# Attention values stored unscaled beside their reciprocals, gathered rows scaled before the transposes, and a new order of the attention

## Chip, cores and metric

The kernel runs on one core of a Trainium2 chip. The metric is the device time of one execution in microseconds; the median of three runs is compared. TensorE runs at one of two clock levels, 1.2 or 2.4 GHz; the profile gives the granted clock as a share of 2.4.

## What is computed

Eight batches of eight heads: 512 tokens x and 32 state rows attend to each other, both ways. The results are rows of 512 numbers (4608 rows). Each row goes to one of eight experts, greedily by its gate logits with room for 576 rows in each, and then through a gated network that all rows share:

```python
xread = np.matmul(softmax(scale * x @ state.T), state)
sread = np.matmul(softmax(scale * state @ x.T), x)
logits = x @ w_gate
out[mask] = np.maximum(x[mask] @ w1[e], 0.0) @ w2[e]
return (silu(x @ w_gate) * (x @ w_val)) @ w_out
```

The softmax divides by its sum plus 1e-9.

## The kernel before

The attention is written as 343 short steps, each a function of a batch (and a half or quarter); the string ORDER lists them, `name.batch`, and a loop issues them so that each step's instructions stand behind those of the step before on every engine:

```python
    for op in ORDER.split():
        name, b = op.split(".")
        in_order(DO[name], int(b))
```

The names: x (TensorE transposes a quarter of the tokens) and ax (its copy into xT, by VectorE or ScalarE as X_VECTOR says); p, ap and q, aq (state and its gate columns; aq copies into SC); z (scores), m, n, y, o (maxima and block transposes); c or C (subtraction of the row maximum, zc, on POOL or VectorE); e, E and f (exponentials of the two softmaxes); t, at (transposes of one of them); r, ar (token values into px, copied to xu with their sums and gate parts); s (state values), S0 (sum plus 1e-9 and reciprocal, rd), S1 (scaled state values ss, stored to DRAM by SP); d (reciprocals of the token sums), M (token values times reciprocals into xm, in two halves on POOL, then stored to xm_d by SP, line 429), w (gate logits of the tokens into Lw, on POOL); G, aG, GG, aGG (transposes of ss, copy into TS, gate products of the state rows, copy into Lw). Batch 7 is read in two halves (A, B1, l0, LB, l1, w1). N, I and cnt make the keys of all 34 columns of 128 rows, the comparison table for the first digit in five pieces (CHUNKS), and its 34 products. The values of batches 7 and 6 are scaled behind the list by ScalarE, 64 instructions (lines 487 to 507).

Then `search` and `place` find, digit by digit, which rows go to the first expert, and write their numbers to idx. POOL gathers these rows from xm_d, five tiles of up to 128 rows (line 916); TensorE transposes each tile (`turn`, line 925), ScalarE and VectorE split it into a high and a low part xh, xl (lines 930 and 931). The first expert's weights come from DRAM as soon as its number is known; ScalarE makes their high parts (line 1132), VectorE the remainders (line 1142); beside them VectorE makes the keys of the next search. Twenty products of no use run on TensorE in between (`spin`).

The experts take 128 units, 16 to an expert: twelve products into one of two PSUM tiles h, an activation on ScalarE (hh, line 950), a remainder on VectorE (hl, line 951), and twelve products of an earlier unit. A table `plan` says at which unit other work is issued: the selection for the next expert, its weights, gathers ("g"), transposes ("t"). Instructions of one engine then run in the order in which the compiler's scheduler puts them within such pins (`issue_after`). Behind the experts the shared network runs for the rest of the time.

## Time and profile before

| | us |
|---|---|
| median of three runs | 1329.91 |
| lowest and highest | 1327.9, 1331.71 |
| the profiled execution | 1332.65 |
| its span, first to last instruction | 1330.9 |
| TensorE busy in the span | 1289.3 (97%) |
| VectorE, ScalarE, POOL busy | 1039.9, 544.0, 409.4 |

The rows below are from this one execution. A group of instructions has its line, engine, operation, output and inputs, the count, the busy time with the mean in ns, and behind a bar the engine's idle time ahead of it with what ended it. In a timeline the first number is the start in us from the span's start, the second the duration, and the square bracket is the idle time ahead and its releaser. PE is TensorE, DVE VectorE, ACT ScalarE; line 245 stands for all steps of the attention, which one helper records.

### The profile page before, as it was taken

To read this page: it belongs to the slowest core of one execution; us is meant where nothing else is said; L and a number is where in the kernel's file an instruction comes from. 1 tells how busy PE (TensorE), PEld (TensorE's weight loads), DVE (VectorE), ACT (ScalarE), POOL (GpSimd) and SP (SyncE) were. 2 spreads that over 40 slices of the span, in tenths; PEclk is the share of its full clock that TensorE was granted. 3 is DMA by queue.
4 is the path that set the end of the run, shared out by engine and by line. 5 is a ranking of instruction groups with operands and counts; after the bars stand their busy time and mean duration, and the time that the engine had idled before them with its cause. 6 is when DMAs were issued, how large, how long until landed. Compare 5 with 4: busy or idle time off the path is not lost.

```text
span 1330.9 us, 28488 instructions
## 1 busy us (share of the span) xinstructions
PE 1289.3 (97%) x11113; PEld 1253.9 (94%) x11113; DVE 1039.9 (78%) x2040; ACT 544.0 (41%) x1047; POOL 409.4 (31%) x349
## 2 busy tenths in 40 slices
...
GB/s 185 225 127 168 119 98 219 150 117 216 155 138 153 198 142 195 93 269 214 161 175 172 285 212 206 278 234 204 293 180 202 176 239 129 172 170 133 131 124 64
DMA packets 129782, 236.97 MB, mean 178 GB/s; under 512 B 29168, under 2 KB 55792, under 8 KB 128624
## 3 DMA queue, kind: packets, MB, share of 16 engines
...
## 4 chain that ended last, share of the span: by engine, by line
PE 90%; DVE 5%; DMA 2%; ACT 1%; issue 1%; SPq 0%; POOLq 0%; DVEq 0%; ACTq 0%
PE b L1257 53%; PE h L946 15%; PE y L962 5%; PE y L965 5%; PE y L961 5%; PE pt L245 2%; PE px L245 2%; PE bt L925 1%; PE acc L642 1%; DMA xc<-in_x_dram 1%; DMA yr<-m_d 1%; PE z L245 1%; PE acc L734 0%; DMA raw<-in_moe_w_dram 0%; DVE m L1307 0%
## 5 line engine op out<-in xcount | busy, mean ns | idle before, releaser
L1257 PE MATMUL b<-yb,w 128*128 128x364 f32 (+1 forms) x3024 | 500.5, 327 | 1.7 <-DVE m L1303 1.5
L1257 PEld LDWEIGHTS b<-yb,w 128*128 128x128 f32 x3024 | 499.5, 188 | 2.6 <-DVE m L1303 2.1
L1257 PE MATMUL b<-w,yb 128*128 128x256 f32 x2160 | 256.3, 281 | 0.9 <-ACT yb L986 0.6
L1257 PEld LDWEIGHTS b<-w,yb 128*128 128x128 f32 x2160 | 255.7, 188 | 1.4 <-ACT yb L986 0.9
L946 PE MATMUL h<-xh,w 128*128 128x288 f32 (+1 forms) x1024 | 207.9, 295 | 1.5 <-ACT xh L930 1.2
L946 PEld LDWEIGHTS h<-xh,w 128*128 128x128 f32 x1024 | 161.6, 189 | 2.5 <-ACT xh L930 1.8
L916 POOL DMA_INDIRECT xg<-xm_d,idx x38 | 49.6, 1304 | 354.6 <-PE bt L925 155.7
L946 PE MATMUL h<-xl,w 128*128 128x288 f32 (+1 forms) x512 | 147.8, 291 | 0.5 <-DVE xl L931 0.5
L961 PE MATMUL y<-hh,w 128*128 128x288 f32 (+1 forms) x512 | 136.0, 291 | 0.1
L962 PE MATMUL y<-hh,w 128*128 128x288 f32 (+1 forms) x512 | 135.7, 291 | 0.0
L950 ACT ACTIVATE hh<-h 128x288 fp32r<-128x288 f32 (+1 forms) x128 | 50.9, 398 | 187.8 <-PE h L946 176.4
L1304 ACT ACTIVATE m<-m 128x364 f32<-128x364 f32 (+1 forms) x108 | 54.8, 507 | 156.5 <-DVE m L1303 151.1
L987 DVE TENSOR_TENSOR yb<-ty,yb 128x512 fp32r<-128x512 f32 (+2 forms) x96 | 92.0, 964 | 12.8 <-ACT yb L986 10.9
L961 PEld LDWEIGHTS y<-hh,w 128*128 128x128 f32 x512 | 96.5, 189 | 0.3 <-ACT hh L950 0.3
L946 PEld LDWEIGHTS h<-xl,w 128*128 128x128 f32 x512 | 96.0, 188 | 0.9 <-DVE xl L931 0.9
L962 PEld LDWEIGHTS y<-hh,w 128*128 128x128 f32 x512 | 96.5, 189 | 0.0
L951 DVE SCALAR_TENSOR_TENSOR hl<-h,hh 128x288 fp32r<-128x288 f32 (+1 forms) x128 | 55.7, 436 | 50.2 <-ACT hh L950 49.8
L1014 POOL TENSOR_TENSOR tt<-raw 128x512 f32<-128x512 f32 (+1 forms) x23 | 30.8, 1341 | 207.3 <-DMA raw<-m_d 154.6
L986 ACT CAST yb<-ty 128x512 fp32r<-128x512 f32 (+2 forms) x96 | 66.6, 694 | 56.5 <-PE b L1257 28.7
L965 PE MATMUL y<-hl,w 128*128 128x288 f32 (+1 forms) x512 | 88.0, 290 | 0.0
L987 DVE TENSOR_TENSOR yb<-yr,yb 128x512 fp32r<-128x512 f32 (+2 forms) x73 | 75.6, 1037 | 10.0 <-ACT yb L986 9.3
L1307 DVE TENSOR_TENSOR m<-cv,m 128x364 f32<-128x364 f32 (+1 forms) x108 | 68.9, 638 | 9.6 <-ACT m L1304 0.2
...
## 6 DMA issues: line engine op xcount, KB each, us to landing
...
```

Of the source, the lines that this page charges most:

```text
L245: done = getattr(getattr(nc, self.name), op)(*args, **kwargs)
L946: hooks["p"] = nc.tensor.matmul(ph, W[i][0][k][q == 1][:, fs], (xl if q == 2 else xh)[:, k, :T], start=(n == 0), stop=(n == 11)).ins
L950: relu[16 * i + 8 * hf + f] = hooks["hh"] = nc.scalar.activation(hh, ph, AF.Relu).ins
L951: lower[16 * i + 8 * hf + f] = hooks["h"] = nc.vector.scalar_tensor_tensor(hl, ph, 0.0, f32(hh), op0=OP.max, op1=OP.subtract).ins
L961: nc.tensor.matmul(p[d], wh[:, f % 2, ds_], hh, start=(f == 0), stop=False)
L962: nc.tensor.matmul(p[d], wl[:, f % 2, ds_], hh, start=False, stop=False)
L965: nc.tensor.matmul(p[d], wh[:, f % 2, ds_], hl, start=False, stop=(f == 7))
L986: nc.scalar.copy(hi, src)
L987: nc.vector.tensor_tensor(lo, src, f32(hi), OP.subtract)
L1257: nc.tensor.matmul(out, a, b, skip_group_check=True, start=start and n == 0, stop=stop and n == len(terms) - 1)
L1304: hooks["silu"] = nc.scalar.activation(m[:, l], m[:, l], AF.Silu).ins
L1307: hooks["gate"] = nc.vector.tensor_tensor(m[:, l], c, m[:, l], OP.mult).ins
```

## The change

Rows of xm_d become 8 x 73 numbers instead of 8 x 64: a head's 64 unscaled values, the reciprocal of its sum in the place of the sum, and its eight gate parts. The steps M and the 64 instructions behind the list go; d stores the whole tile xu, of which there are four now. State rows are stored scaled as before, with ones beside them (one9). Gathered tiles have 584 columns and are multiplied by their reciprocals before the transposes (`scale_rows`): the first expert's first two by VectorE, all others by ScalarE in eight instructions each. The plan issues gathers of tiles 3 and 4 and the transposes at other units. The sum plus 1e-9 of the state rows goes from S0 to a step V on POOL; aq and aG go from ScalarE to VectorE; for batches 1 to 7 the ax of the last quarter (ax3) goes from VectorE to ScalarE. K makes the keys of the first 24 columns, T0 to T2 three pieces of the table, kc their 24 products; N, I and cnt do the rest. The list has a new order. The first expert's weight remainders are pinned ahead of and between the two VectorE scalings, the next keys behind them.

```diff
@@ -51,26 +51,26 @@
-X_VECTOR = (1, 3)
+X_VECTOR = (1,)
 ORDER = """
...
-x0.7 f0.6 at0.5 f1.6 c0.6 c1.6 ax3.7 ax0.7 S0.5 e0.6 r0.5 S0.6 t0.6 e1.6 ar0.5 z.7 m.7 r1.5 E.6 at0.6
-s0.5 y1.7 t1.6 y0.7 ar1.5 M0.4 s1.5 n.7 w.4 d.5 r0.6 S1.5 at1.6 G.5 f0.7 aG.5 o1.7 C1.7 e1.7 o0.7
-s0.6 t0.7 ar0.6 f1.7 M1.4 s1.6 S1.6 S0.7 r1.6 C0.7 GG.3 aGG.3 at0.7 M1.5 t1.7 E1.7 ar1.6 at1.7 s0.7 M0.5
-A1.7 e0.7 s1.7 G.6 d.6 S1.7 w.5 E0.7 B1.7 w.6 G.7 l1.7 w1.7 A0.7 aG.6 aG.7 GG.7 l0.7 LB.7 aGG.7
-N.7 I.7 cnt.7
...
+x3.6 at0.4 G.2 aG.2 x2.6 x0.6 n.5 ax3.6 ax2.6 o.5 ax0.6 f1.5 f0.5 c1.5 x1.6 r0.4 c0.5 ax1.6 V.4 q.6
+x0.7 aq.6 ax0.7 G.3 e1.5 aG.3 w.1 z.6 q.7 e0.5 m.6 ar0.4 S0.4 t1.4 aq.7 y.6 r1.4 o.6 s0.4 E.5
+at1.4 w.2 x1.7 s1.4 ar1.4 S1.4 n.6 V.5 c1.6 x3.7 ax1.7 f1.6 ax3.7 x2.7 ax2.7 t0.5 G.4 d.3 r0.5 c0.6
+e1.6 f0.6 d.4 at0.5 z.7 aG.4 e0.6 ar0.5 E.6 t1.5 at1.5 t0.6 y1.7 at0.6 r1.5 w.3 m.7 w.4 s0.5 t1.6
+s1.5 y0.7 o0.7 ar1.5 S0.5 at1.6 o1.7 S1.5 n.7 f1.7 d.5 r0.6 V.6 c0.7 c1.7 e0.7 GG.3 ar0.6 aGG.3 s0.6
+G.5 w.5 s1.6 f0.7 e1.7 aG.5 r1.6 E0.7 E1.7 ar1.6 S0.6 S1.6 K.7 t0.7 V.7 at0.7 d.6 T0.7 t1.7 T2.7
+A1.7 s0.7 at1.7 B1.7 S0.7 G.6 w.6 s1.7 l1.7 S1.7 A0.7 G.7 aG.6 T1.7 aG.7 GG.7 kc.7 l0.7 w1.7 LB.7
+aGG.7 N.7 I.7 B0.7 cnt.7
@@ -87,7 +87,7 @@
     dram = ctx.enter_context(tc.tile_pool(name="dram", bufs=1, space=bass.MemoryType.DRAM))
-    xm_d = dram.tile([N, DM], F32, name="xm_d")
+    xm_d = dram.tile([N, H * ROW], F32, name="xm_d")
@@ -136,6 +136,8 @@
     nc.gpsimd.memset(SC[:, :, :, D:D + 1], 1.0)
+    one9 = ac.tile([32, H, ROW - D], F32, name="one9")
+    nc.gpsimd.memset(one9, 1.0)
@@ -278,7 +280,7 @@
     def prep_gate2(b):
-        an.scalar.copy(SC[:, b, :, D + 1:], st[b]["q"][:, :2 * E].rearrange("p (g e) -> p g e", g=2))
+        an.vector.tensor_copy(SC[:, b, :, D + 1:], st[b]["q"][:, :2 * E].rearrange("p (g e) -> p g e", g=2))
@@ -406,28 +408,23 @@
     def xread2(b, half):
...
         if "xu" not in t:
-            t["xu"] = aw.tile([128, 4, H, ROW], F32, name="xu", bufs=3)
+            t["xu"] = aw.tile([128, 4, H, ROW], F32, name="xu", bufs=4)
...
+    def row_store(b, xu, dst):
+        nc.sync.dma_start(dst, xu.rearrange("p r h c -> p r (h c)"))
+    def token_rows(b):
+        return xm_d[b * SE:b * SE + S].rearrange("(p r) c -> p r c", r=4)
     def xscale(b):
         xu = st[b]["xu"]
-        rd = st[b]["rd"] = aw.tile([128, 4, H], F32, name="rd", bufs=2)
+        rd = aw.tile([128, 4, H], F32, name="rd", bufs=2)
         an.vector.tensor_scalar(rd, xu[:, :, :, D], 1e-9, None, op0=OP.add)
-        an.vector.reciprocal(rd, rd)
-    def xmake(b, j):
-        t = st[b]
-        xu, rd = t["xu"], t["rd"]
-        done = "xm" in t
-        if not done:
-            t["xm"] = aw.tile([128, 4, H, D], F32, name="xm")
-        xm, q = t["xm"], slice(2 * j, 2 * j + 2)
-        an.gpsimd.tensor_tensor(xm[:, q], xu[:, q, :, :D], rd[:, q, :, None].to_broadcast([128, 2, H, D]), OP.mult)
-        if done:
-            nc.sync.dma_start(xm_d[b * SE:b * SE + S].rearrange("(p r) c -> p r c", r=4),
-                              xm.rearrange("p r h d -> p r (h d)"))
+        an.vector.reciprocal(xu[:, :, :, D], rd)
+        row_store(b, xu, token_rows(b))
     def add_heads(b, xw):
@@ -435,9 +432,9 @@
     def logits(b):
-        xu, rd = st[b]["xu"], st[b]["rd"]
+        xu = st[b]["xu"]
         xw = aw.tile([128, 4, H, E], F32, name="xw")
-        an.gpsimd.tensor_tensor(xw, xu[:, :, :, D + 1:], rd[:, :, :, None].to_broadcast([128, 4, H, E]), OP.mult)
+        an.gpsimd.tensor_tensor(xw, xu[:, :, :, D + 1:], xu[:, :, :, D:D + 1].to_broadcast([128, 4, H, E]), OP.mult)
...
     def read_half(b, j):
@@ -451,8 +448,8 @@
     def keep_half(b):
         t = st[b]
-        t["xh"] = aw.tile([128, 2, H, ROW], F32, name="xu", bufs=3)
-        an.scalar.copy(by_row(t["xh"]), by_bank(t["h", 1]))
+        t["xh", 1] = aw.tile([128, 2, H, ROW], F32, name="xu", bufs=4)
+        an.scalar.copy(by_row(t["xh", 1]), by_bank(t["h", 1]))
     def half_logits(b, j):
@@ -470,41 +467,30 @@
     def gates_sum(b):
...
+    def half_store(b, j):
+        row_store(b, st[b]["xh", j], token_rows(b).rearrange("p (k j) c -> p j k c", j=2)[:, j])
     def kept_scale(b):
-        t = st[b]
-        rd = t["rd", 1] = aw.tile([128, 2, H], F32, name="rd1", bufs=1)
-        an.vector.tensor_scalar(rd, t["xh"][:, :, :, D], 1e-9, None, op0=OP.add)
-        an.vector.reciprocal(rd, rd)
+        xh = st[b]["xh", 1]
+        rd = aw.tile([128, 2, H], F32, name="rd1", bufs=1)
+        an.vector.tensor_scalar(rd, xh[:, :, :, D], 1e-9, None, op0=OP.add)
+        an.vector.reciprocal(xh[:, :, :, D], rd)
+        half_store(b, 1)
     def kept_logits(b):
-        t = st[b]
+        xh = st[b]["xh", 1]
         xw = aw.tile([128, 2, H, E], F32, name="xw")
-        an.gpsimd.tensor_tensor(xw, t["xh"][:, :, :, D + 1:],
-                                t["rd", 1][:, :, :, None].to_broadcast([128, 2, H, E]), OP.mult)
+        an.gpsimd.tensor_tensor(xw, xh[:, :, :, D + 1:], xh[:, :, :, D:D + 1].to_broadcast([128, 2, H, E]), OP.mult)
...
-    def scale_values(b):
+    def values_half(b):
         t = st[b]
-        xm = aw.tile([128, 4, H, D], F32, name="xm")
-        for j in range(2):
-            for k in range(2):
-                for h in range(H):
-                    m = 2 * k + h // 4
-                    v = t["h", 0][:, h % 4, ROW * m:ROW * m + D] if j == 0 else t["xh"][:, k, h, :D]
-                    an.scalar.activation(xm[:, 2 * k + j, h, :], v, AF.Copy, scale=t["rd", j][:, k, h:h + 1])
-        nc.sync.dma_start(xm_d[b * SE:b * SE + S].rearrange("(p r) c -> p r c", r=4),
-                          xm.rearrange("p r h d -> p r (h d)"))
-    def scale_kept(b):
-        xu, rd = st[b]["xu"], st[b]["rd"]
-        xm = aw.tile([128, 4, H, D], F32, name="xm")
-        for r in range(4):
-            for h in range(H):
-                an.scalar.activation(xm[:, r, h, :], xu[:, r, h, :D], AF.Copy, scale=rd[:, r, h:h + 1])
-        nc.sync.dma_start(xm_d[b * SE:b * SE + S].rearrange("(p r) c -> p r c", r=4),
-                          xm.rearrange("p r h d -> p r (h d)"))
+        xh = t["xh", 0] = aw.tile([128, 2, H, ROW], F32, name="xu", bufs=4)
+        an.scalar.copy(by_row(xh), by_bank(t["h", 0]))
+        an.scalar.copy(xh[:, :, :, D], t["rd", 0])
+        half_store(b, 0)
     def sread(b, g):
@@ -519,10 +505,13 @@
...
+    def state_sum(b):
+        den = st[b]["den"] = aw.tile([128, 2], F32, name="den")
+        an.gpsimd.tensor_scalar(den, st[b]["den2"][:, :, 0], 1e-9, None, op0=OP.add)
     def state_scale(b):
         rd2 = st[b]["rd2"] = aw.tile([128, 2], F32, name="rd2")
-        an.vector.tensor_scalar(rd2, st[b]["den2"][:, :, 0], 1e-9, None, op0=OP.add)
-        an.vector.reciprocal(rd2, rd2)
+        an.vector.reciprocal(rd2, st[b]["den"])
     def sread2(b):
@@ -532,8 +521,9 @@
         for h in range(4):
-            dst = xm_d[r0:r0 + NS].rearrange("n (g h d) -> n g h d", g=2, h=4)[:, :, h, :]
+            dst = xm_d[r0:r0 + NS].rearrange("n (g h c) -> n g h c", g=2, h=4)[:, :, h, :D]
             nc.sync.dma_start(dst, ss[32 * h:32 * h + 32])
+        nc.sync.dma_start(xm_d[r0:r0 + NS].rearrange("n (h c) -> n h c", h=H)[:, :, D:], one9)
...
     def sread_gate(b):
@@ -542,7 +532,7 @@
     def sread_gate2(b):
-        an.scalar.copy(TS[:, :, b, :], st[b]["g"][:, :128].rearrange("p (h n) -> p h n", h=4))
+        an.vector.tensor_copy(TS[:, :, b, :], st[b]["g"][:, :128].rearrange("p (h n) -> p h n", h=4))
     def state_gates(b):
@@ -808,20 +798,35 @@
...
+    EARLY_COLUMNS = 24
+    held = {}
+    def early_keys(b):
+        keys(0, EARLY_COLUMNS, True, an)
+        sl["I"] = sel_tile([128, 128 * NC], BF, "I").rearrange("p (g j c) -> p g j c", j=128, c=2)
+    def table(b, j):
+        pairs(sl["I"], 1, Dms[0], *CHUNKS[j], OP.is_le, an)
+    def counts(c0, c1):
+        for c in range(c0, c1):
+            an.tensor.matmul(held["acc"], sl["I"][:, c // 2, :, c % 2], G[:, c, :], start=(c == 0), stop=(c == NC - 1))
+    def early_counts(b):
+        held["acc"] = ap.tile([128, 2, 512], F32, name="z")[:, 0, :E]
+        counts(0, EARLY_COLUMNS)
     def first_keys(b):
-        keys(0, NC, True, an)
+        keys(EARLY_COLUMNS, NC, True, an)
     def first_table(b):
-        sl["I"] = sel_tile([128, 128 * NC], BF, "I").rearrange("p (g j c) -> p g j c", j=128, c=2)
-        for c0, c1 in CHUNKS:
-            pairs(sl["I"], 1, Dms[0], c0, c1, OP.is_le, an)
+        table(b, 3)
+        table(b, 4)
     def first_count(b):
-        acc = ap.tile([128, 2, 512], F32, name="z")[:, 0, :E]
-        for c in range(NC):
-            an.tensor.matmul(acc, sl["I"][:, c // 2, :, c % 2], G[:, c, :], start=(c == 0), stop=(c == NC - 1))
+        counts(EARLY_COLUMNS, NC)
         fe = sl["fe"] = sel_tile([128, E], BF, "fe")
-        an.vector.tensor_tensor(fe, acc, need, OP.is_ge)
+        an.vector.tensor_tensor(fe, held["acc"], need, OP.is_ge)
     def halves(fn, *more):
@@ -829,11 +834,12 @@
           "GG": state_gates, "aGG": state_gates2, "B1": keep_half, "l0": gates_read, "LB": gates_sum,
-          "l1": kept_scale, "w1": kept_logits, "N": first_keys, "I": first_table, "cnt": first_count}
+          "l1": kept_scale, "w1": kept_logits, "N": first_keys, "I": first_table, "cnt": first_count,
+          "B0": values_half, "V": state_sum, "K": early_keys, "kc": early_counts}
...
                            ("t", turn_e2, ()), ("at", turn_e2b, ()), ("s", sread, ()), ("e", exps1, ()),
-                           ("E", exps1b, ()), ("r", xread, ()), ("ar", xread2, ()), ("M", xmake, ()),
+                           ("E", exps1b, ()), ("r", xread, ()), ("ar", xread2, ()), ("T", table, ()),
@@ -842,8 +848,6 @@
             load_x(int(b) + 4)
-    in_order(scale_values, B - 1)
-    in_order(scale_kept, B - 2)
...
@@ -908,17 +913,27 @@
         if i or j < 3:
-            xg = gx.tile([128, DM], F32, name="xg", bufs=3)
+            xg = gx.tile([128, H * ROW], F32, name="xg", bufs=3)
...
             if j == 3:
-                XG["ys"] = bw.tile([128, 4, 288], F32, name="ys", bufs=1).rearrange("p (a b) c -> p a (b c)", a=2)
-            xg = XG["ys"][:, j - 3, :DM]
+                XG["ys"] = bw.tile([128, 4, 292], F32, name="ys", bufs=1).rearrange("p (a b) c -> p a (b c)", a=2)
+            xg = XG["ys"][:, j - 3]
...
                                      in_offset=bass.IndirectOffsetOnAxis(ap=idx[i][:n, j:j + 1], axis=0)).ins
-        XG[i, j] = xg
+        XG[i, j] = xg.rearrange("p (h c) -> p h c", c=ROW)
+    def scale_rows(i, j, eng=None):
+        n = min(128, CAP - 128 * j)
+        xg = XG.pop((i, j))[:n]
+        xs = XS[i, j] = gx.tile([128, H, D], F32, name="xs", bufs=5)
+        if eng is not None:
+            hooks["scaled"] = eng.tensor_tensor(xs[:n], xg[:, :, :D], xg[:, :, D:D + 1].to_broadcast([n, H, D]), OP.mult).ins
+            return
+        for h in range(H):
+            nc.scalar.activation(xs[:n, h, :], xg[:, h, :D], AF.Copy, scale=xg[:, h, D:D + 1])
     def turn(i, j):
-        xg = XG.pop((i, j))
+        xg = XS.pop((i, j)).rearrange("p h d -> p (h d)")
...
@@ -1135,16 +1150,22 @@
         close(0, bpsum)
-    with tc.issue_after(hooks["lw"]):
-        keys(0, NC, False)
-    with tc.issue_after(hooks["key"]):
-        for k in range(4):
-            nc.vector.tensor_tensor(lo[k], first[k], f32(hi[k]), OP.subtract)
+    def first_lower(k, pin):
+        with tc.issue_after(hooks[pin]):
+            hooks["low"] = nc.vector.tensor_tensor(lo[k], first[k], f32(hi[k]), OP.subtract).ins
...
         spin(bp, "y2", 1, P_["spin"])
+    first_lower(0, "lw")
+    first_lower(1, "low")
     for j in range(2):
+        with tc.issue_after(hooks["low"]):
+            scale_rows(0, j, nc.vector)
+        first_lower(2 + j, "scaled")
         turn(0, j)
+    with tc.issue_after(hooks["low"]):
+        keys(0, NC, False)
@@ -1190,10 +1211,13 @@
         for j in range(NT):
-            at(P_["g"][k] + int(j * P_["gs"]), P_["ghook"], gather, k, j)
+            turned = P_["t"][k] + j + 2 * (k == E - 1) if k > 1 else 14 + j + 2 * (j > 2)
+            at(P_["g"][k] + int(j * P_["gs"]) if j < 3 else P_["t"][k] + j - 3 if k > 1 else 17, P_["ghook"] if j < 3 else None, gather, k, j)
+            at(max(turned - 2, P_["g"][k] + 2) if k > 1 else 12 + j if j < 3 else turned - 1, "hh", scale_rows, k, j)
             if k > 1 or j > 1:
-                at(P_["t"][k] + j, P_["thook"], turn, k, j)
+                at(turned, P_["thook"], turn, k, j)
     for j in range(2, NT):
+        at(P_["t0"][j - 2] - 2, "hh", scale_rows, 0, j)
```

## Rows read from the trace of the kernel before

**Rows 1.** Busy time by stretch: TensorE, weight loads, VectorE, ScalarE, POOL, granted clock.
```profile
16.00:77.00 61.00, 57.45 (x1397) 44.75 (x1398) 54.23 (x87) 50.46 (x102) 45.24 (x47) 1.00 0.53 176
77.00:86.00 9.00, 8.90 (x141) 7.50 (x139) 3.10 (x13) 6.37 (x21) 3.89 (x11) 0.52 0.37 133
200.00:300.00 100.00, 100.00 (x990) 97.28 (x990) 82.60 (x219) 36.60 (x65) 11.79 (x10) 1.00 0.48 161
```

**Rows 2.** Groups of VectorE's instructions, 14 to 86 us.
```profile
L245 DVE TENSOR_SCALAR rd<-den 128x2 f32<-128x2 f32 x8 | 5.0, 631 | 0.0
L245 DVE COPY xT<-px 128x512 f32<-128x512 f32 x7 | 4.8, 681 | 1.8 <-ACT e L245 0.7 <-ACT xT L245 0.6 <-ACT nmx L245 0.3
```

**Rows 3.** Groups of POOL's instructions, same stretch.
```profile
L245 POOL TENSOR_TENSOR xm<-xu,rd 128x1024 f32<-128x1024 f32 x12 | 23.4, 1957 | 4.0 <-ACT xT L245 2.6 <-ACT e L245 0.8 <-ACT et L245 0.6
```

**Rows 4.** Groups of ScalarE's instructions, same stretch.
```profile
L245 ACT COPY xT<-px 128x512 f32<-128x512 f32 x7 | 4.1, 589 | 3.0 <-PE px L245 2.9
L245 ACT COPY TS<-pt 128x128 f32<-128x128 f32 x8 | 2.1, 265 | 0.8 <-PE pt L245 0.8
```

**Rows 5.** TensorE's waits, 14 to 90 us: total, times, longest in us.
```profile
PE px L245 <- ACT xT L245: 1.1, 2, 0.7
PE px L245 <- ACT xu L245: 0.9, 3, 0.4
...
PE pt L245 <- DVE ss L245: 0.8, 2, 0.5
...
PE pt L245 <- ACT TS L245: 0.5, 1, 0.5
PE pt L245 <- ACT SC L245: 0.4, 1, 0.4
```

**Rows 6.** Timeline of TensorE near the attention's end: steps s, r and GG.3.
```profile
72.36 0.65 PE L245 MATMUL pt<-xc,et 128*32 128x64 f32 x32
...
74.12 1.13 PE L245 MATMUL px<-SC,e 32*128 32x73 f32 x32
75.78 1.06 PE L245 MATMUL pt<-wgp,TS 128*128 128x8 f32 x8 [0.53 <-DVE ss L245]
```

**Rows 7.** Timeline of VectorE behind the attention: first keys, first table.
```profile
86.22 0.43 DVE L245 TENSOR_REDUCE V<-Lw 128x34 f32<-128x272 f32 x1
...
88.65 2.69 DVE L245 TENSOR_TENSOR I<-IE,Dm 128x1024 bf16<-128x1024 bf16 x5
```

**Rows 8.** Timeline of ScalarE behind the attention: scaling of the last values.
```profile
88.40 8.74 ACT L245 ACTIVATE xm<-xu,rd 128x64 f32<-128x64 f32 x36
```

**Rows 9.** Timeline of POOL: issues of gathers, three of expert 0, one of expert 3.
```profile
113.14 1.18 POOL L916 DMA_INDIRECT xg<-xm_d,idx  x1 [29.53 <-DVE eh L751]
114.62 1.13 POOL L916 DMA_INDIRECT xg<-xm_d,idx  x1 [0.31 <-issue]
116.06 5.77 POOL L916 DMA_INDIRECT xg<-xm_d,idx  x1 [0.30 <-issue]
...
252.83 0.96 POOL L916 DMA_INDIRECT xg<-xm_d,idx  x1 [22.18 <-issue]
```

**Rows 10.** DMA issues, 113 to 114.5 us: median us from issue to landing.
```profile
xg<-xm_d,idx POOLq DMA_INDIRECT x1, 3.6
```

**Rows 11.** Timeline of VectorE behind the first row numbers: Lw, four remainders.
```profile
113.45 0.44 DVE L757 TENSOR_TENSOR Lw<-Lw,dn 128x272 f32<-128x272 f32 x1
...
116.38 4.62 DVE L1142 TENSOR_TENSOR w<-raw,w 128x1024 fp32r<-128x1024 f32 x4
```

**Rows 12.** Timeline of TensorE: the first expert's first products.
```profile
119.58 2.16 PE L946 MATMUL h<-xh,w 128*128 128x256 f32 x16 [0.68 <-ACT xh L930]
122.25 1.20 PE L946 MATMUL h<-xl,w 128*128 128x256 f32 x8 [0.50 <-DVE xl L931]
```

**Rows 13.** Line 950, one activation to a unit: ns, first and last start in us.
```profile
L950 ACT ACTIVATE hh<-h x128: 372/392/417, 123.1 to 558.3; 128x256 fp32r<-128x256 f32 x64, 128x288 fp32r<-128x288 f32 x64
```

**Rows 14.** Groups of ScalarE's instructions, 119 to 500 us.
```profile
L873 ACT CAST w<-raw 128x1024 fp32r<-128x1024 f32 x45 | 46.0, 1049 | 17.5 <-PE y L965 11.9 <-DMA raw<-in_moe_w_dram 3.7 <-PE acc L771 1.2
```

26 lines of the change are left out of this document (12 added, 14 removed).

## The prediction

> **What bounds the kernel now.** I read the busy times by stretch first, then TensorE's waits inside the attention, then the timelines around the attention's end and the start of the first expert. [rows 1] show three kinds of stretch. From 200 to 300 us TensorE is busy without a gap (100.00 of 100) while ScalarE has 36.60: there only TensorE's own work counts, and this change leaves that work as it is. In the attention TensorE is busy too, but from 16 to 77 it idles 61.00 − 57.45 = 3.55 us. From 77 to 86 it is busy for 8.90 of 9 us, but the granted clock is 0.52, its lower level of 1.2 GHz: work that needs about 4.45 us at 2.4 GHz. Behind 86 comes a chain of small steps without cover: keys and first table on VectorE [rows 7], the search, the placing, the gathers [rows 9], the first hidden products at 119.58 [rows 12]. So a microsecond counts in four places: TensorE's idle time in the attention, its clock at the attention's end, the keys and the table, and the way from the row numbers to the first product.
>
> **The attention's body.** POOL loses twelve halves of the scaling, 23.4 us [rows 3], about half of the 45.24 us that it is busy from 16 to 77 [rows 1]. VectorE loses the small additions rd<-den, 5.0 us at 631 ns each [rows 2], long for two numbers a row because they stand beside POOL's long multiplications; they go to POOL. It also loses seven copies into xT at 0.68 us [rows 2], 4.8 us, which ScalarE takes over at 0.589 [rows 4], 4.1 us. The last batch's two zc (C1.7 and C0.7 in the list) go from VectorE to POOL as well. ScalarE gives VectorE eight copies into TS at 0.265 us [rows 4] and eight smaller ones into SC, some 3.5 us together. So ScalarE stays as full as it was (50.46 of 61 us), VectorE ends some 6 us lighter (54.23 now). What TensorE waits for stands in [rows 5]: ss (0.8 us), TS (0.5) and SC (0.4) are VectorE's works, or become so, and VectorE gets room: I count these 1.7 us as gone. Of the waits on xT and xu (1.1 and 0.9), copies of ScalarE, whose load doesn't fall, I count half, 1.0 us, since such a copy is often late through VectorE and POOL. Together −2.7 us. The ends are −3.55 (all idle time) and +2: xT is the longest of those waits already, and if each of the seven new xT copies in ScalarE's queue delays TensorE by half its 0.589 us, that is 2 us. What is late next there is a copy of ScalarE.
>
> **Stores.** The unscaled tile is stored at its reciprocal's place, so SP waits for VectorE instead of POOL, and what is queued behind it on SP, the loads of later x among it, gets no later. Each batch adds one store of ones for the state rows, and rows grow from 512 to 584 numbers. All of it has to be there only at the first gather at 113.14 [rows 9], 27 us behind the attention: 0. Without that cover a last store would cost a landing, about the 3.6 us of [rows 10]. The 64 small multiplications of the last two batches leave ScalarE; the last 36 take 8.74 us from 88.40 [rows 8] and end 16 us ahead of the gather, so that is worth 0 as well.
>
> **Keys and table.** Now VectorE does the keys of all 34 columns from 86.22 to 88.65, 2.43 us, and the table in five pieces, 2.69 us [rows 7]. Then 24 columns, three pieces and their products are done early. Left are the keys of 10 columns, which I take at 1.4 us (the ends are 10/34 of 2.43, or 0.7, and all of it, since each operation has a fixed part), and one whole and one quarter piece, about 0.75 us against 2.69. That is −1.0 − 1.9 = −2.9 us; ends −3.6 (24/34 of 5.12) and 0, if the early part is itself late. The early part costs VectorE about 1.7 + 1.6 = 3.3 us. VectorE's idle time at the attention's end hides it: busy 3.10 of 9 us there [rows 1], 5.9 free. If TensorE became faster there, this cover would shrink, and up to those 3.3 us would come back.
>
> **From row numbers to the first product.** Before, the second tile is fetched from 114.62 and lands 3.6 us later [rows 9, 10], at 118.2; the product starts at 119.58 [rows 12], 1.36 us behind it. Now VectorE comes between, in an order that is written out: two weight remainders, tile 0, a remainder, tile 1, the last remainder, and the next expert's keys only then. A remainder costs 4.62 / 4 = 1.15 us [rows 11]; for the scaling no row exists, and I take 0.7 us, as the attention's copies of the same 128 x 512 (0.68, [rows 2]), with the remainder's 1.2 as the other end. The first remainder starts behind the update of Lw, at 113.85 [rows 11], so two are done at 116.15; tile 0 lands at 113.14 + 3.6 = 116.74, is scaled by 117.44, the third remainder done by 118.57, tile 1 by 119.27. Plus 1.36: 120.63, 1.05 us later than now. But all remainders are done by 120.4 instead of 121.0, and the wait of 0.50 us before 122.25 [rows 12] goes: net +0.55 us.
>
> The risk lies on POOL. An undisturbed gather issues in 0.96 us; the third one took 5.77, until just behind four remainders in a row [rows 9, 11]. So remainders can hold up an issue, and now two of them run beside the second gather's. If it waits for both (116.15), needs its 0.96 us and then the 2.4 us from the end of an issue to landing (3.6 − 1.18), tile 1 lands at 119.5 and the product starts at 121.55: +1.5 us net. If it is held through the third remainder too, +3.9. I take 1.0, between the first two, because VectorE has a gap of 0.6 us behind the second remainder while it waits for tile 0.
>
> The Trainium skill's page "SBUF — State Buffer", section "Who interferes with whom", says that a VectorE tensor_tensor with both inputs in SBUF takes only the shared read interface, and infers that descriptor generation needs the write side and is not stalled by it. By it this term would be 0.55 and not 1.0; the row of 5.77 us beside such remainders speaks against it.
>
> The next expert's keys move from ahead of the remainders to behind them, 2.4 us of VectorE work that now runs beside products. Expert 1's row numbers are needed at unit 16, 16 x 3.43 = 55 us later (a unit is (558.3 − 123.1) / 127 = 3.43 us, [rows 13]): 0, and what exceeds that slack if it is used up.
>
> **The experts.** ScalarE gets 38 tiles of eight multiplications: 8 x 8.74 / 36 = 1.94 us each, five to an expert of 16 x 3.43 = 55 us: 9.7 us, or 17.7 per 100 on top of 36.60 [rows 1]. A tile is mostly scaled two units (6.9 us) ahead of its transposes, and TensorE has a unit's other products to do while one activation is late. The gathers of tiles 3 and 4 start when a scaled tile is free, not when a transposed one is, which is earlier. I take +0.3 us for a few late activations; the ends are 0 and the rival's price below.
>
> **Sum.** −2.7 − 2.9 + 1.0 + 0.3 = −4.3 us. The profiled execution took 1332.65 us with a span of 1330.9, 2.7 us over the median of the three runs shown, 1329.91. Against its own time the sum gives 1328.35; against the median, the figure to compare, 1325.6.
>
> **Rivals.** *The clock holds.* In the old order the gates of the first state rows (eight tiny products in 1.06 us) stand behind a gap of 0.53 us at 75.78 [rows 6], and soon behind them the clock is down [rows 1]. With fewer gaps it may stay up to the end: 8.9 us at half speed become 4.45, another −4.4, so 1321.2. Against it: the end still has only small products, and the early keys would lose cover.
>
> *The clock falls sooner.* In the new list those gates have s0.6, G.5, s1.6, r1.6 and t0.7 behind them that stood ahead before: about 0.65 + 0.3 + 0.65 + 1.13 + 0.65 = 3.4 us at full clock (s and r in [rows 6], t taken as s). If the fall comes as long after the gates as before, these run at half speed: +3.4, so 1329.0, no change.
>
> *Slower: ScalarE becomes the bound of the experts.* Place: the five units (17.1 us) in which an expert's tiles are scaled. The average load is 0.366 x 17.1 = 6.3, with the scaling 16.0 of 17.1; if four casts of weights more than the average fall there (4.2 us at 1.05, [rows 14]), the backlog is 3.1 us. It decides from the point where an activation is later than the one unit that TensorE has in hand, or where a gather that is not yet there holds ScalarE's queue. If half of 3.1 reaches TensorE in each of seven experts: +11 on the sum, so 1336.5. For it: TensorE has no gap to give there. Against it: 63% of ScalarE is free on average.
>
> *It does not do what it says:* TensorE's waits stay, because ScalarE's queue makes them: without the −2.7, 1328.3.
>
> **Chances.** Forecast 0.45 (own range 1323 to 1329), clock holds 0.27, clock sooner 0.13, ScalarE 0.10, no relief 0.05. The low end, 1319.5, is the held clock with all idle time gone (1321.2 − 0.85) and a gather term near its lower end; the high end, 1332.5, takes in the gather's +3.9 or the body's +2, one with a smaller gain on the keys, and leaves out most of the ScalarE case. What a measurement can tell from no change is 0.3%, 4.0 us, so a time below 1325.9 counts as faster: nearly all of the held clock and half of the forecast, 0.48; slower (above 1333.9) are the ScalarE case and a sum of mishaps, 0.12; the rest is 0.40.
>
> **What would show it.** Right: rd<-den gone from VectorE; TensorE idle for about 1 us in the attention's body; the first keys and table behind the last Lw some 3 us shorter; the first product about 7.9 us behind the first gather's issue instead of 119.58 − 113.14 = 6.4; and still no gap in TensorE from 200 to 300. Wrong: a clock at its lower level for clearly less or more than 9 us at the attention's end; a second gather of over 3 us; TensorE idle behind ScalarE in the experts; a body whose idle time stays at 3.5 us.

## The result, and the profile after

The changed kernel takes 1345.66 us (median of 6 runs, 1342.14 to 1352.8), the kernel before in the same session 1329.54 us (6 runs, 1327.9 to 1331.71): 1.0126 times as long, with a 95% interval of 1.0097 to 1.0154. That is 16 us slower where 4 us faster were forecast, and outside the range. The profiled execution took 1343.6 us, with a span of 1341.5 us; the runs of the changed kernel also spread over 10 us, those of the kernel before over 4. The two profiled executions are only 10.95 us apart (1343.6 - 1332.65), that of the changed kernel 2.1 us below its median and that of the kernel before some 3 above its own, so the traces can account for 11 of the 16 us and not for the rest.

The first view is the busy time by stretch of the changed kernel: length, then TensorE, weight loads, VectorE, ScalarE and POOL (each with its count of instructions), then the granted clock, DMA share and GB/s.

```profile
16.00:77.00 61.00, 57.33 (x1402) 45.86 (x1402) 49.91 (x94) 52.76 (x99) 27.50 (x48) 1.00 0.62 199
77.00:86.00 9.00, 6.57 (x172) 5.70 (x173) 7.59 (x32) 3.43 (x5) 3.94 (x8) 0.81 0.74 278
...
120.00:205.00 85.00, 79.29 (x752) 75.82 (x751) 63.09 (x189) 38.82 (x109) 7.62 (x5) 0.92 0.28 91
200.00:300.00 100.00, 100.00 (x988) 96.86 (x987) 81.83 (x237) 51.61 (x138) 13.22 (x10) 1.00 0.51 167
345.00:430.00 85.00, 82.63 (x801) 79.51 (x800) 66.84 (x193) 44.31 (x119) 6.67 (x8) 1.00 0.45 151
```

The same two later stretches of the kernel before:

```profile
120.00:205.00 85.00, 82.99 (x854) 79.24 (x853) 70.76 (x218) 27.48 (x48) 12.39 (x8) 1.00 0.40 137
345.00:430.00 85.00, 85.00 (x811) 83.07 (x810) 64.94 (x190) 29.21 (x55) 7.94 (x8) 1.00 0.52 165
```

The attention did well. Its body idles as before (61.00 - 57.33 = 3.67 us, where [rows 1] give 3.55), but its end is shorter: the mean clock from 77 to 86 is 0.81 instead of 0.52. VectorE's last copy into Lw, which ends the attention, and the comparison of the first count, in the kernel before and in the changed one:

```profile
85.95 0.17 DVE L245 COPY Lw<-pt 128x8 f32<-128x8 f32 x1 [0.50 <-PE pt L245]
...
91.66 0.17 DVE L245 TENSOR_TENSOR fe<-z,need 128x8 bf16<-128x8 f32 x1
```

```profile
83.26 0.17 DVE L247 COPY Lw<-pt 128x8 f32<-128x8 f32 x1 [0.29 <-PE pt L247]
...
86.14 0.17 DVE L247 TENSOR_TENSOR fe<-z,need 128x8 bf16<-128x8 f32 x1
```

The attention ends 2.69 us sooner, and keys and table take 2.88 us behind it instead of 5.71, another 2.83. So the first count is compared 5.5 us sooner, and the first row numbers are written at 107.18 instead of 112.67. From 200 to 300 TensorE has no gap, as before, though ScalarE went from 36.60 to 51.61.

The loss lies between. From 120 to 205 TensorE idles 85.00 - 79.29 = 5.71 us (before 2.01), and the clock is 0.92 instead of 1.00, which over 85 us is 6.8 us of lost work. Together that is some 10.5 us more than before. From 345 to 430 another 2.37 us of idle time are new. The stores of the finished halves of the experts' outputs tell the same: the first is 4.0 us later than before (157.70 against 153.66 us), the second 9.1 (190.46 against 181.34), the tenth 12.0 (426.40 against 414.38).

Where it starts is in three timelines of the changed kernel, each start, duration, engine, line, operation, with the idle time before it and its releaser in brackets. VectorE, POOL and SP's queue behind the row numbers:

```profile
107.18 0.17 DVE L730 TENSOR_TENSOR idx<-dp 128x5 int32<-128x5 f32 x1
...
108.30 2.35 DVE L1155 TENSOR_TENSOR w<-raw,w 128x1024 fp32r<-128x1024 f32 x2
112.02 0.69 DVE L930 TENSOR_TENSOR xs<-xg 128x512 f32<-128x512 f32 x1 [1.36 <-DMA xg<-xm_d,idx]
112.63 1.22 DVE L1155 TENSOR_TENSOR w<-raw,w 128x1024 fp32r<-128x1024 f32 x1
116.73 0.69 DVE L930 TENSOR_TENSOR xs<-xg 128x512 f32<-128x512 f32 x1 [2.88 <-DMA xg<-xm_d,idx]
...
117.94 1.22 DVE L1155 TENSOR_TENSOR w<-raw,w 128x1024 fp32r<-128x1024 f32 x1
```

```profile
108.24 1.23 POOL L921 DMA_INDIRECT xg<-xm_d,idx  x1 [26.01 <-DMA raw<-in_moe_w_dram]
109.76 1.71 POOL L921 DMA_INDIRECT xg<-xm_d,idx  x1 [0.30 <-issue]
```

```profile
109.55 0.40 SPq L891 DMA_DIRECT2D raw<-in_moe_w_dram  x1
110.69 0.38 SPq L891 DMA_DIRECT2D raw<-in_moe_w_dram  x1
113.87 0.37 SPq L891 DMA_DIRECT2D raw<-in_moe_w_dram  x1
119.27 0.37 SPq L891 DMA_DIRECT2D raw<-in_moe_w_dram  x1
```

The scaling itself costs 0.69 us, as taken. The second gather is issued from 109.76, but its tile is there only at 116.73, 7.0 us later (before 3.6, [rows 10]). The four loads of the second weights, 512 KB each, are issued as the remainders end: the second at 110.69 behind 108.30 + 2.35 = 110.65, the third at 113.87 behind 113.85, the last at 119.27 behind 119.16. Before, the first was issued at 117.62, now at 109.55, and three of the four are issued before the second gather's tile is there. Then TensorE, only rows with a wait:

```profile
117.48 1.11 PE L940 MATMUL y<-ident,xs 128*128 128x128 f32 x4 [4.06 <-DVE xs L930]
119.27 2.72 PE L961 MATMUL h<-xh,w 128*128 128x256 f32 x11 [0.68 <-ACT xh L945]
129.21 0.17 PE L761 MATMUL acc<-crb,onesb 128*128 128x8 bf16 x1 [1.14 <-DVE crb L759]
130.01 1.03 PE L611 MATMUL acc<-G,I 128*128 128x8 bf16 x34 [0.64 <-DVE need L762]
...
173.36 0.53 PE L961 MATMUL h<-xh,w 128*128 128x288 f32 x2 [1.21 <-DVE hl L966]
183.37 0.99 PE L611 MATMUL acc<-G,I 128*128 128x8 bf16 x34 [2.17 <-DVE need L762]
```

and one row of ScalarE:

```profile
170.50 2.02 ACT L933 ACTIVATE xs<-xg 128x64 f32<-128x64 f32 x8 [5.11 <-DMA xg<-xm_d,idx]
```

So the first product is at 119.27, only 0.3 us sooner than before (119.58, [rows 12]), though the row numbers were 5.5 us sooner. At 129 TensorE stands at products of the second search, whose keys now come behind the remainders. At 165.4 ScalarE begins to stand 5.11 us at the scaling of expert 1's first tile, which has not landed; the activations behind it in its queue, then VectorE's hl and need, then TensorE (173 and 183) are late. That tile's gather is issued from 163.36 and there at 170.5, 7.1 us later, with two loads of second weights issued beside it (165.06 and 167.17). In the kernel before, the three gathers at this place took 6.3 us (median) and no copy of ScalarE stood behind them: its tiles were not needed before their transposes. Behind the waits that end at 117.48, 130.01 and 183.37 the clock is at its lower level for a while (behind that of 1.21 us at 173.36 it is not), by stretches of the same kernel:

```profile
120.00:125.00 5.00, 5.00 (x31) 5.00 (x30) 3.62 (x10) 2.17 (x6) 0.00 (x0) 0.65 0.38 105
...
130.00:135.00 5.00, 4.99 (x53) 4.89 (x53) 4.97 (x16) 1.58 (x5) 0.00 (x0) 0.54 0.00 0
185.00:190.00 5.00, 4.98 (x38) 4.58 (x37) 2.75 (x11) 1.28 (x3) 0.00 (x0) 0.66 0.01 3
```

### The profile page after: what moved, and what is told of

It reads as the page before. It is cut to its first block, busy times and chain, and to the rows that moved or that the text cites. A ratio compares the mean times of both kernels' runs of the same rounds, so it can differ in the third digit from the quotient of the medians.

```text
span 1341.5 us, 28724 instructions
## 1 busy us (share of the span) xinstructions
PE 1289.7 (96%) x11112; PEld 1255.5 (94%) x11113; DVE 1033.8 (77%) x2050; ACT 600.3 (45%) x1280; POOL 386.1 (29%) x348
## 4 chain that ended last, share of the span: by engine, by line
PE 53%; DMA 1%; DVE 1%; issue 0%; ACT 0%; POOLq 0%; DVEq 0%; SPq 0%
PE b L1281 53%; DMA yr<-m_d 1%; DVE yb L1002 0%; DMA m_d<-m 0%; ACT yb L1001 0%; DVE m L1327 0%; DVE u L1339 0%; DMA mt_d<-m 0%; POOLq L1617 0%; DVE m L1346 0%; DVE m L1331 0%; DVE cv L1330 0%; ACT m L1328 0%; DVEq L1346 0%; DVEq L1327 0%
## 5 line engine op out<-in xcount | busy, mean ns | idle before, releaser
L921 POOL DMA_INDIRECT xg<-xm_d,idx x38 | 44.9, 1182 | 373.2 <-ACT xs L933 135.1
L933 ACT ACTIVATE xs<-xg 128x64 f32<-128x64 f32 (+1 forms) x288 | 74.5, 338 | 5.2 <-DMA xg<-xm_d,idx 5.1
```

The source lines that it names most:

```text
L921: hooks["g"] = nc.gpsimd.indirect_dma_start(out=xg[:n], out_offset=None, in_=xm_d, in_offset=bass.IndirectOffsetOnAxis(ap=idx[i][:n, j:j + ...
L933: nc.scalar.activation(xs[:n, h, :], xg[:, h, :D], AF.Copy, scale=xg[:, h, D:D + 1])
```

## The experiments

Theory A: the order of the work around the first products is wrong in three places (remainders that start loads beside the gather, late keys, a scaling that holds ScalarE's queue), and the clock doubles what each costs. Its rivals blame the work itself: the scaling's load, the longer rows, POOL's port. Unless the text says otherwise, each kernel is the changed one with that edit; of some edits only the main lines are shown. Times are medians; the kernel before stood at 1328.88 to 1330.52 in the sessions.

**Scalings first.** Tile 0 and 1 are scaled ahead of all remainders.

```
-    first_lower(0, "lw")
-    first_lower(1, "low")
     for j in range(2):
-        with tc.issue_after(hooks["low"]):
+        with tc.issue_after(hooks["lw" if j == 0 else "scaled"]):
             scale_rows(0, j, nc.vector)
-        first_lower(2 + j, "scaled")
         turn(0, j)
+    first_lower(0, "scaled")
+    for k in range(1, 4):
+        first_lower(k, "low")
```

> After, with tile 0 and tile 1 of expert 0 scaled ahead of the four weight remainders, and the next expert's keys last as in after. Theory A (the remainders, being first, free the raw buffers, so the four 512 KB loads of the next weights start at 109.55 us and share the DMA engines with the second gather): these loads start behind the second tile's landing, that gather lands about 3.6 us behind its issue (113.4) instead of 7.0, the first product is at about 115.5 instead of 119.27, TensorE's wait of 4.06 us behind the spin goes, and the time falls by 4 to 6 us, to 1340 to 1342. Rival B (the gather is late by itself, through the longer rows of 584 numbers or through the two scalings on VectorE): the second gather still lands 5 to 7 us behind its issue, and the time stays within 2 us of after's 1345.7. In both the stalls at the products of the second search (129 to 131) stay, since the keys are still late.

Measured: 1340.31 us (1339.3 to 1341.33), 5.3 us less. The four loads start at 115.41, the second tile is scaled at 113.55, 3.6 us behind its gather's issue at 109.91, and the first product is at 115.63. As theory A has it; B falls. Its profiled execution (1341.33 us) is only 2.3 us below that of the changed kernel; the rest of the 5.3 us lies in executions without a trace.

**Keys first**, then the scalings, then the remainders: the edit above, with "key" in the place of "lw", and

```
+    with tc.issue_after(hooks["lw"]):
+        keys(0, NC, False)
     second_tiles(0, eid)
...
-    with tc.issue_after(hooks["low"]):
-        keys(0, NC, False)
```

> After, with the next expert's keys first (as before), then the two scalings, then the four remainders. Theory A (late keys let TensorE's in-order queue stand at the products of the second search, 1.14 and 0.64 us, with the clock low behind them, and the row numbers of expert 1 come 3.5 us later): the gain of the run with the scalings first and 3 to 5 us more, so 1335 to 1339; the waits on crb and need near 130 gone, expert 1's first gather issued back near 52 us behind the first row numbers (before 159.83 - 112.7 = 47, after 163.36 - 107.2 = 56). Rival B (the place of the keys costs nothing, as the prediction had it): the same as the run with the scalings first, within 1.5 us. Rival C (the keys ahead of the scaling delay the first product by their 2.4 us): slower than the run with the scalings first by 1 to 2 us.

Measured: 1338.44 us (1337.03 to 1341.29), 1.9 us below the scalings first. The wait on crb is gone and expert 1's first gather is issued at 157.23, but need near 175 (2.2 us) and ScalarE's 4.98 us stay. In the trace the first half's store is at 151.59 instead of 155.02, 3.4 us sooner. In the time four runs each don't separate the two (1.0072 and 1.0077 of before, intervals 1.0054 to 1.0090 and 1.0060 to 1.0093), so A's mechanism is seen and its size is not; C falls, B (within 1.5 us) isn't excluded by the times.

**The scaling on POOL** for all tiles but the first two:

```
-        for h in range(H):
-            nc.scalar.activation(xs[:n, h, :], xg[:, h, :D], AF.Copy, scale=xg[:, h, D:D + 1])
+        nc.gpsimd.tensor_tensor(xs[:n], xg[:, :, :D], xg[:, :, D:D + 1].to_broadcast([n, H, D]), OP.mult)
```

> After, with all tiles but the first two scaled by POOL in one multiplication instead of eight activations of ScalarE. Theory A (ScalarE's in-order queue stands 5.1 us at the scaling of a late tile of expert 1 at 170.5 us, so that its activations, then VectorE and TensorE are late, some 5 us near 175 to 190): the loss between the stores of the first and the second half expert 1 goes, -4 to -6 us, to 1340 to 1342; ScalarE's wait on xg near 170 gone. Rival D (ScalarE's load of 1.94 us a tile, in every expert, is what costs): the gain comes in all experts, some 1 to 1.5 us in each. Rival E (expert 1 is late because its row numbers are, not because of ScalarE; and POOL's multiplication of 4 us holds POOL's own gathers and takes VectorE's port): no gain, or slower by up to 5 us.

Measured: 1347.29 us (1345.93 to 1349.19), no gain. The stretch of expert 1 got 2.5 us shorter (its store at 187.93 instead of 190.46), but POOL's own queue now stands at the late tile, and from 332 to 341 new stalls with a low clock took that back. E's sign. Taking 74.5 us of scaling off ScalarE gains nothing, which speaks against D, though POOL's new stalls are mixed into it.

**A longer spin**: 42 instead of 20 of the products that only keep TensorE busy.

```
-        spin(bp, "y2", 1, P_["spin"])
+        spin(bp, "y2", 1, 42)
```

> After, with 42 instead of 20 products that only keep TensorE busy before the first expert. Theory A (the 4.06 us of idle time behind the spin let the granted clock fall, 0.65 from 120 to 125, so the first products run at the lower level): with some 22 more spin products of 0.2 us the idle time is filled, the clock stays up at 120 to 125, and the time falls by 2 to 3 us, to about 1343. Rival B (the lower clock there is the same as before's and costs nothing, because VectorE's remainders and copies set that stretch): no change, within 1 us. If the spin ends later than the first operand it delays the first product by that much: up to +1.

Measured: 1336.48 us (1334.01 to 1340.09), 9.2 us less, three times the 2 to 3 us expected, though the first product came 2.2 us later, at 121.43 (1.2 of them because the row numbers did, at 108.42). One stretch of it:

```profile
120.00:205.00 85.00, 83.14 (x862) 79.64 (x861) 72.58 (x224) 42.78 (x114) 5.67 (x5) 1.00 0.36 120
```

Idle time fell from 5.71 to 1.86 us and the clock holds: 3.9 + 6.8 us, less the 2.2, is 8.5. The gap fillers did more than fill the gap: the units start later, so that the second search's products and expert 1's first tile are in time (ScalarE waits 0.49 us for it, not 5.11). That tile also comes sooner: its gather is issued at 157.77 instead of 163.36, and it is there 4.0 us later instead of 7.1.

**32 of them**, to part the two.

> After, with 32 products that only keep TensorE busy instead of 20 (42 gave 1336.5, with the first product 2.2 us later than in after). Theory A1 (those 42 helped through the granted clock and the filled gap): with 32 the spin ends about when the second tile is scaled, the first product is at about 119.3 as in after, the clock stays up from 113 to 125, and the time is 1341 to 1343, since ScalarE still stands at expert 1's tile. Theory A2 (they helped because the units of expert 0 start later and at a full clock, so that the row numbers of expert 1, which come by their own chain, are in time): then 32 gives little, 1344 to 1346.

Measured: 1340.41 us (1337.89 to 1345.09). The first product is at 117.96, the clock 1.00 from 113 to 125, and ScalarE stands 4.2 us at expert 1's tile again. By these medians clock and gap give about 5 us and the later units about 4 more, so that A1 and A2 both hold in part. But the four runs spread over 7 us (interval 1.0054 to 1.0124 of before, against 1.0036 to 1.0070 with 42), so this split is an estimate.

**Expert 1's scaling two units later**, first in the run with the keys first, then alone:

```
-            turned = P_["t"][k] + j + 2 * (k == E - 1) if k > 1 else 14 + j + 2 * (j > 2)
+            turned = P_["t"][k] + j + 2 * (k == E - 1) if k > 1 else 14 + j + 2 * (j > 1)
...
-            at(max(turned - 2, P_["g"][k] + 2) if k > 1 else 12 + j if j < 3 else turned - 1, "hh", scale_rows, k, j)
+            at(max(turned - 2, P_["g"][k] + 2) if k > 1 else 14 + j if j < 3 else turned - 1, "hh", scale_rows, k, j)
```

> The run with the next keys first and the scalings ahead of the remainders (1338.4), and in it the scalings of expert 1's tiles 0, 1 and 2 moved two units later in ScalarE's list, to units 14, 15 and 16 instead of 12, 13 and 14 (tile 2's transposes two units later with it). Theory A (ScalarE's in-order queue stands behind a tile that has not landed, 4.98 us at 164.8 us of that run): that wait goes, the 4.2 us that this run loses against before between its stores at 151.59 and 183.43 go, and the time is 1333.5 to 1335. Rival D (the work of the scaling itself, 2 us a tile, is what costs): 1338, within 1 us. Rival F (expert 1's tiles are then late for their own transposes at unit 16): the wait moves from ScalarE to TensorE, and the time stays or gets worse by 1 to 3 us.

> After, with only the scalings of expert 1's tiles 0, 1 and 2 moved two units later. Theory A: the 5.11 us wait of ScalarE at 170.5 goes, and with it the 5.1 us lost between the stores at 157.70 and 190.46: 1340 to 1342. Rival D: 1345 to 1346, no change.

Measured: 1334.54 us (1331.51 to 1339.58), 3.9 us below the keys first, and alone 1339.34 us (1336.59 to 1341.47), 6.3 us below the changed kernel. In neither is ScalarE's wait for the tile among its waits any more; the work is the same. So the scaling costs through its place in the queue, not by its 2 us a tile: A, and D falls again.

**The early keys undone**: K.7, T0.7, T2.7, T1.7 and kc.7 leave the list, and all of it stands in N, I and cnt.

```
     def first_keys(b):
-        keys(EARLY_COLUMNS, NC, True, an)
+        early_keys(b)
     def first_table(b):
-        table(b, 3)
-        table(b, 4)
+        for j in range(5):
+            table(b, j)
...
-        counts(EARLY_COLUMNS, NC)
+        held["acc"] = ap.tile([128, 2, 512], F32, name="z")[:, 0, :E]
+        counts(0, NC)
```

with `keys(0, NC, True, an)` in `early_keys`.

> After, with the early keys undone: the keys of all 34 columns, the five pieces of the first table and all 34 counts stand behind the attention again, as in before; the rest of the new attention stays. By the prediction's term the early part is worth 2.9 us: the first row numbers come at about 110.2 instead of 107.3, and the time is 1347.5 to 1349. Theory A has the gain before the row numbers, 5.5 us in all, made up of these 2.9 us and of a clock that falls later: the clock's 2.6 us stay. Rival G (VectorE's early work itself held the attention's end, and the order alone made the 5.5 us): row numbers at 107 to 108.5, no change in the time.

Measured: 1344.73 us (1342.71 to 1350.95), where 1347.5 to 1349 was expected. Last copy into Lw, first count and row numbers of this run, on VectorE:

```profile
82.38 0.17 DVE L247 COPY Lw<-pt 128x8 f32<-128x8 f32 x1
...
88.10 0.17 DVE L247 TENSOR_TENSOR fe<-z,need 128x8 bf16<-128x8 f32 x1
...
109.16 0.17 DVE L730 TENSOR_TENSOR idx<-dp 128x5 int32<-128x5 f32 x1
```

Keys and table take 5.72 us behind the attention, as before the change, and 2.88 with the early part: it is worth 2.84 us there. At the row numbers 2.0 us of it are left (109.16 - 107.18), because this execution's attention ended 0.88 us sooner. Whether the early work makes that difference, as G has it, stays open: in the 16 profiled executions that share the changed kernel's attention the row numbers lie between 106.13 and 108.42. A's split of the 5.5 us was about right. That the time didn't move says little: with runs that spread over 8 and 10 us, a difference of 2 us can't be seen.

**The second weights behind the gathers**, by POOL's queue; the remainders still come first:

```
-    second_tiles(0, eid)
+    second_tiles(0, expert_id(0, nc.gpsimd), nc.gpsimd)
...
```

> After, with only this changed: the four loads of expert 0's second weights are issued from POOL's queue, behind the five gathers, instead of from SP's. The remainders still come first. Theory A1 (the early loads are what makes the second gather late): the second tile lands some 3.5 us behind its issue plus the 0.75 us that a remainder holds the issue, near 113.5 to 114.3 instead of 116.73, the first product is at 116 to 117, and the time is 1341 to 1344; the second weights come later, which can cost up to 1 us at the first unit's end. Theory A2 (the remainders on VectorE make it late, through the issue's descriptors): it still lands near 116.5, no gain.

POOL, VectorE and TensorE of this run:

```profile
108.74 1.72 POOL L921 DMA_INDIRECT xg<-xm_d,idx  x1 [0.30 <-issue]
...
114.74 3.02 POOL L891 DMA_DIRECT2D raw<-in_moe_w_dram  x4
```

```profile
112.89 0.69 DVE L930 TENSOR_TENSOR xs<-xg 128x512 f32<-128x512 f32 x1 [0.16 <-DMA xg<-xm_d,idx]
```

```profile
114.97 1.58 PE L961 MATMUL h<-xh,w 128*128 128x256 f32 x11 [0.68 <-ACT xh L945]
```

With the loads alone moved, the second tile is there 4.15 us behind its issue, and the first product 8.82 us behind the row numbers (106.15 here) instead of 12.09. So it is the loads that made it late; the remainders cost the issue 0.77 us (1.72 here and 1.71 in the changed kernel, 0.95 where the scalings come first) and no more. The time is 1345.96 us, but its four runs spread from 1337.43 to 1350.7, so what this alone is worth stays open. In its profile the store at 187.06 is 3.4 us sooner than the changed kernel's (its row numbers are 1.0 sooner), and the last of the sixteen only 0.5 (573.79 against 574.28), with the clock at 0.96 from 345 to 430.

**Scalings of experts 2 to 7 one unit earlier**, on the kernel with keys first and expert 1 shifted (1334.54):

```
-            at(max(turned - 2, P_["g"][k] + 2) if k > 1 else 14 + j if j < 3 else turned - 1, "hh", scale_rows, k, j)
+            at(max(turned - 3, P_["g"][k] + 2) if k > 1 else 14 + j if j < 3 else turned - 1, "hh", scale_rows, k, j)
```

> The run with the keys first and expert 1's scalings two units later (1334.5), and in it the scalings of experts 2 to 7 one unit earlier in ScalarE's list (three units ahead of their transposes instead of two). With it the 34 products that place expert 5's rows stand in TensorE's list as in before, behind the first products of the next half, not ahead of the last products of the half before. Theory A (these products, standing too early, hold TensorE's in-order queue for 1.82 us behind VectorE's rh near 356 us, and the clock is low for 3.5 us behind that, 1.7 us): the wait goes, -3 to -3.5 us, so 1331 to 1332. Rival H (that wait only takes the place of one that comes later anyway): 1334 to 1335.

Measured: 1332.27 us (1330.2 to 1334.5), 2.3 us less. The 34 products that place expert 5's rows (line 724) stood ahead of a half's last products in TensorE's list and waited 1.82 us for rh; now they stand behind the next half's first, as before, and from 345 to 430 TensorE is without a gap. The order within the pins is the compiler's, and moving ScalarE's new work by one unit brought the old one back. A holds in kind; its gain is 2.3 us by these medians and 3.9 against the kernel before of each session (from 5.7 above it to 1.7), where 3 to 3.5 were expected. H falls.

**On top of that**, with 26 spin products; with expert 1's tiles only one unit later; and the kernel with 42 and both shifts of the scaling:

> The same with 26 instead of 20 products that only keep TensorE busy, which fill the gaps of 0.24 and 1.03 us ahead of the second tile's transposes. Theory A (the granted clock, 0.77 from 113 to 120 and 0.64 from 120 to 125 in the run without them, takes 3.3 us from the first products when it falls): the clock stays at 1.00 there, and the time is 0 to 3 us below the same kernel with 20, depending on how often its runs lose the clock, with less spread; if the spin ends late it costs up to 1 us.

> As the run with experts 2 to 7 one unit earlier, but expert 1's tiles scaled one unit later than in after (units 13, 14, 15) instead of two. Theory A (the gather of its first tile lands near 165, about at unit 13's activation; two units are more than it needs and bring tile 1's transposes close to their use, 0.64 and 0.79 us of TensorE's waits at 179 to 181 with 1.7 us of clock behind them): 1 to 3 us less, if ScalarE's wait on the tile is under 1.5 us; if that wait is still above 2 us, no change or slower by 1.

> The run with 42 spin products and after's order (remainders first, keys last; 1336.5), with both shifts of the scaling added. Theory A: its only large wait, 1.82 us at 355 with 1.7 us of clock, goes: 1333 to 1334; expert 1's shift gives nothing here, since its tile is in time in that run. Rival H: 1336.

Measured: 1331.10 us (1329.8 to 1334.14), a gain of 1.2 that its runs don't separate from none; 1334.76 us (1332.68 to 1338.68), 2.5 us slower where 1 to 3 us of gain were expected; 1333.97 us (1331.08 to 1335.67), as expected. The miss shows how narrow the place is: one unit is too early, ScalarE still waits 2.85 us for the tile, and TensorE with it.

```profile
175.63 1.02 PE L611 MATMUL acc<-G,I 128*128 128x8 bf16 x34 [1.74 <-DVE need L762]
```

**All mends together**, on the run with 26 spin products. The remainders go one behind each scaling, the transposes of expert 1's first tiles to either side of a half's last products, and the first units' terms are reordered. Then the same with 20 spin products, and the transposes alone:

```
-            terms.sort(key=lambda kq: kq[1])
+            terms.sort(key=lambda kq: (0, 2, 1)[kq[1]])
...
+            turn(1, 0)
             expert_out(*pend.pop(0))
-            for j in range(2):
-                turn(1, j)
+            turn(1, 1)
```

> All mends together, on the run with 26 spin products (1331.1): besides, one remainder stands behind each of the two scalings, the first two units take the products with the remainder of x ahead of those with the remainder of the weights, and expert 1's first two tiles are transposed one on each side of the last products of expert 0. If what is left are the waits seen in that run (1.24 and 0.63 us on the weights' remainders, 0.64 and 0.80 us at expert 1's first products, and 1.7 us of clock behind the first): 2 to 4 us less, 1327 to 1329.5, so below before by 0.1 to 0.3%. If these waits cover later ones: 1330 to 1331, the same as before.

> All mends together with 20 spin products instead of 26. The first product comes some 0.7 us sooner, at about 115.5 instead of 116.3; if the granted clock holds in the gaps of some 1 us ahead of it, 0.5 us less than with 26; if it falls there, as in the run with 20 (4.7 us lost to the clock from 112 to 205), 2 to 3 us more.

> The run with 26 spin products (1331.1), with only the transposes of expert 1's first two tiles moved, one on each side of the last products of expert 0. If TensorE's 0.64 and 0.80 us near 180 are due to the two transposes standing together: 1 to 1.5 us less, 1329.5 to 1330. If not: 1331.

Measured: 1330.59 us (1328.81 to 1332.38; ratio to before 1.0007, interval 0.9997 to 1.0018), 1330.44 us (1328.3 to 1337.13) and 1331.95 us (1329.31 to 1335.35). The first of them has the clean stretch that was aimed at:

```profile
120.00:205.00 85.00, 83.95 (x866) 80.64 (x866) 71.55 (x213) 43.97 (x117) 8.31 (x5) 1.00 0.38 130
```

That is less idle time than before had (1.05 against 2.01 us), and the time is the same as before's, not 2 to 4 us below the run with 26, as if these waits had covered later ones. Part of that is seen: 1.2 us of new idle time between 210 and 217, most of it at products of the third search. The moved transposes bring it. Alone they end both waits near 180 (from 120 to 205 TensorE is busy for 84.91 of 85 us), but from 200 to 300 it then idles 1.06 us where the run with 26 had no gap, and the 1 to 1.5 us expected of them don't come. With 20 spin products the clock holds from 113 to 205, but the first product is no sooner than with 26 (116.54 and 116.68), so the two runs don't differ. No version beat the kernel before. In this execution the row numbers are 4.95 us sooner than before (107.72), the first product 2.9 (116.68), and the end of the span 3.0; but the execution of before that was profiled lies 3 us above its own median, so which stretch takes back the rest of the gain can't be read, and stays open. For the same reason the 5.5 us at the row numbers, which rest on this one execution of before, may be less in the median.

## Why the prediction was wrong

*Body of the attention (-2.7): right in size by luck, wrong in its place.* The attention ended 2.69 us sooner, but not through the waits that were to go: the copies moved and rd<-den left VectorE as said, and the body's idle time stayed at 3.67 us, which the prediction had named as a sign of being wrong. What came instead was a part of the rival of the held clock, 0.81 instead of 0.52 at the attention's end. *Keys and table (-2.9): right,* 2.83 behind the last copy into Lw. Together 5.5 us at the row numbers, against 5.6.

*From row numbers to the first product (+1.0, at most +3.9): the first step that failed.* It came to 12.09 us (107.18 to 119.27) instead of 6.91, +5.2. The step costed what the remainders hold on VectorE and on POOL's port, and that part was right: 0.77 us on the issue, 0.69 us a scaling, and with the loads moved away the first product stands 7.76 us behind the first gather's issue, where 7.9 was forecast. It left out what the remainders release: as soon as a remainder is done its raw buffer is free, and SP's queue starts the next 512 KB load, 8 us sooner than before, beside the gather. That is 3.3 us: the loads moved alone brought the 12.09 to 8.82. Another 0.6 lie ahead of the first gather, which is issued 1.06 us behind the row numbers instead of 0.47, and does so within 0.02 us in every version; the profile puts this wait down to a load of the first weights, and no run parts it.

On POOL's port the Trainium skill's page "SBUF — State Buffer", section "Who interferes with whom", infers that a VectorE tensor_tensor with both inputs in SBUF does not stall descriptor generation. Here the traces disagree: an issue takes 1.71 us with remainders beside it, 1.72 where no load of the second weights ran beside it either, and 0.95 without remainders.

*The next keys behind the remainders (0): failed.* The step looked for who needs them at unit 16 and overlooked that TensorE's list carries the second search's products among expert 0's first ones, from 129 us on: waits of 1.14 and 0.64 us, with the clock at 0.54 behind them. With the keys first these waits are gone and the first store is 3.4 us sooner; the time fell by 1.9 us, not clear of the spread of its runs.

*The experts (+0.3, the rival +11): failed, and of the three orders it gives most when mended alone.* The rival had the mechanism in its second condition, a gather that is not yet there and holds ScalarE's queue, but it was priced by ScalarE's load in all seven experts and given 0.10. It happened in expert 1 alone, whose row numbers come just in time. The step took a tile to be scaled two units ahead of its transposes; expert 1's first tile is scaled at unit 12 (`12 + j` in the diff) and transposed at 16, so that ScalarE's queue needs it four units sooner than TensorE does. Moving its scaling by two units gave 6.3 us (the scalings first, alone, 5.3). That ScalarE's load did not matter was right: no gap from 200 to 300.

*What had no term:* the clock behind a stall. From 120 to 205 it took 6.8 us, more than the idle time. And the compiler's other order of expert 5's placing products, 1.82 us of wait near 365 us, of which nothing in the diff warns.

The steps don't add up singly. By medians, scalings first gave 5.3 us, keys 1.9, expert 1's place 3.9, the order near 355 us 2.3, the spin 1.2: 14.6 of the 16.1, though the keys' and the spin's shares are within the spread of their runs. The shift alone gave 6.3 and the spin alone 9.2, since they mend the same stalls.
